# A two-MLP attention kernel: the second MLP takes its wide token groups first and its narrow one last

## The chip, the cores and the metric

The kernel runs on one core of one Trainium2 chip. The metric is the time of one execution on the device in microseconds (us); the median of several runs counts. A profiled execution gives the rows that are shown; its span, from the first to the last instruction, is a little shorter than its own time.

## The reference

Three stages follow each other; only the last one is touched by the change.

```python
def _moe2_ref(x, w1, w2, w3, w_out):
    h = np.maximum(np.maximum(x @ w1, x @ w2), x @ w3)
    return (h @ w_out).astype(np.float32)

def reference(...):
    attn_out = _attn_ref(q, k, v, g_norm)          # linear attention and a norm
    x = attn_out, as 4608 tokens of 512
    x = _moe_ref(x, ...)                           # 512 -> 2048 -> 512, relu squared
    return _moe2_ref(x, ...)                       # 512 -> 768 -> 512, maximum of three products
```

## The kernel before, in words

**Precision.** Every float32 operand of a large product is split into a high and a low part (hilo, line 90: a copy on ScalarE, a subtraction on VectorE), and each product is three matmuls: high by high, high by low, low by high.

**First MLP.** The 4608 tokens are nine tiles of 512 (numbers 0 to 8). A list of slots, one per tile and block of 128 hidden units, is walked in order (line 721). A slot runs u1 (line 337, 12 matmuls into a PSUM bank), u1_end (line 348, ScalarE and VectorE) and, two slots late, u2 (line 359, 12 matmuls into four PSUM banks). Attention for later tiles runs beside it and writes the token tiles xh and xl of pool xp, which has two buffers (x_tile, line 280). The last two tiles, 7 and 8, are walked in two halves of the hidden units: (7, first half), (8, first half), (7, second half), (8, second half). At the end of a half the four banks are added into four staging tiles of pool stp (line 373) and stored to DRAM (line 378, y_dr).

**Between the two.** From the slot where tile 8 begins, "more" (line 748) prepares the second MLP's weights: combine (line 406) makes nine weight tiles of 1792 KB in DRAM (wc_dr), and split_out (line 428) makes six tiles of w_out (wo_dr). They run one after the other through one set of buffers (pool cp), and their last part runs on beside the second MLP.

**Second MLP.** It works on five groups of tokens (SUPERS, line 385): before, the first group is tile 0 as two halves of 256 tokens (the narrow group), then come four groups of two tiles, two halves of 512 tokens each (the wide groups). Products of a pair of 2 by 2 blocks are formed with seven multiplications in place of eight (Winograd's form of Strassen's scheme). For each group there are
- token sums (tok_steps, line 446): 8 loads of y_dr, 14 splits and 8 subtractions, whose results T are read by all nine weight tiles of the group;
- nine steps v1 (line 496), one per weight tile wc: seven products of six matmuls, copies out of PSUM, additions and running maxima, and in every third step the splits of the hidden values hh, hl;
- v2 (line 563): one part per 128 tokens, each of 18 matmuls of width 512, then a copy and a store. The narrow group has four parts, a wide one eight. The first two parts are begun with four of the six hidden blocks, so that the last splits of v1 are covered.

pair_load (line 439) loads one weight tile; each v1 ends with the load for three steps later.

**What sets the order.** A scheduler fixes each engine's order of instructions when the kernel is built, by place in the program and by when it reckons an instruction to be ready. Each engine, and the queue of SP that issues nearly all DMAs, then keeps that order: an instruction whose wait is not over holds up all behind it. A tile that lands on bytes of a closed pool waits only for the users of the old tiles on its own bytes (reuse_waits="tile", line 49).

**Where the tiles lie before.** On the right side of SBUF, on the 64 KB of the first MLP's weights f < 8 (pool wpa, closed at line 752): two weight tiles wc (pool w2a), 14 token tiles (ta) and four load buffers (ya). So pair_load(0) and pair_load(1) are issued in the tail of the first MLP. The third weight tile (pool w2b) and the other token tiles (tb) lie on the left, on bytes that the first MLP holds to its end.

Of the kernel before, what the change touches and what calls it, by code (L numbers as in the profile page):

```python
# [8 lines left out]
F32 = mybir.dt.float32  # L9
F32R = mybir.dt.float32r  # L10
# [10 lines left out]
P = 128  # L21
# [3 lines left out]
def fused_kernel(ctx, tc, qt, kv, kvr, g_norm, w_in, w_out, s, b, w1, w2, w3, w_out2, out):  # L25
    nc = tc.nc
    B, NP, SM, _, _ = kv.shape
# [6 lines left out]
    KD = DM // P  # L34
    KF = DFF // P
    KM = DF2 // P
    TW = 512
    NTILE = NT // TW
# [9 lines left out]
    def pool(name, bufs, space=None, st=ctx, side="left"):  # L48
        kw = {"space": space} if space is not None else {"side": side, "reuse_waits": "tile"}
        return st.enter_context(tc.tile_pool(name=name, bufs=bufs, **kw))  # L50
# [10 lines left out]
    xp = pool("xp", 2, st=mlp1)  # L61
# [21 lines left out]
    HW = DM // 2  # L83
# [6 lines left out]
    def hilo(hi, lo, src):  # L90
        nc.scalar.activation(out=hi, in_=src, func=ACTF.Copy)  # L91
        nc.vector.tensor_tensor(out=lo, in0=src, in1=hi.bitcast(F32), op=ALU.subtract)  # L92


    def w_load(src):
        raw = rawp.tile([P, 2 * DM], U32, tag="raw", name="raw")
        dma(out=raw, in_=src)
        return raw
# [21 lines left out]
    class Weights:  # L120
# [6 lines left out]
        def load(self, cnt):  # L127
            while self.loaded < min(cnt, len(self.need)):
                self.raw[self.loaded] = w_load(self.need[self.loaded][0])
                self.loaded += 1  # L130
# [146 lines left out]
    x_t = {}  # L277
    held = []

    def x_tile(i):  # L280
        if i not in x_t:
            x_t[i] = (
                xp.tile([P, KD, TW], F32R, tag="xh", name="xh"),
                xp.tile([P, KD, TW], F32R, tag="xl", name="xl"),
            )
        return x_t[i]

    def put_x(p, g0, src, n):
        xh, xl = x_tile(g0 // TW)
        o = g0 % TW  # L290
        hilo(xh[:, p, o:o + n], xl[:, p, o:o + n], src)
# [31 lines left out]
    def flush_held():  # L323
        while held:
            p, g0, xo, n = held.pop(0)
            put_x(p, g0, xo[:, :n], n)
# [5 lines left out]
    def y_prev(t):  # L332
        for j in range(KD):
            prev[t, j] = stage()
            dma(out=prev[t, j], in_=y_dr[t][:, j, :])

    def u1(t, o, n, f):
        xh, xl = x_t[t]
        h = ps_h.tile([P, TW], F32, tag="h", name="h")
        w = wi[f].rearrange("p z (a c) -> p z a c", c=P)  # L340
        i = 0
        for kk in range(KD):
            for z, x in ((0, xh), (0, xl), (1, xh)):
                nc.tensor.matmul(h[:, :n], lhsT=w[:, z, kk, :], rhs=x[:, kk, o:o + n], start=(i == 0), stop=(i == 3 * KD - 1))  # L344
                i += 1
        return h
# [35 lines left out]

    A11, A12, A22, S1, S2, S3, S4 = range(7)
    POS = (2, 3, 1, 4, 5, 0, 6)
    SUPERS = [(0, TW // 2)] + [(t, TW) for t in range(1, NTILE, 2)]

    class Plain:

# [48 lines left out]
    wcs, w2p = {}, {}  # L437

    def pair_load(i):
        if i < len(SUPERS) * NQ:  # L440
            wcs[i] = w2p["b" if i % 3 == 2 else "a"].tile([P, 2, 7, HW], F32R, tag="wc", name="wc")
            dma(out=wcs[i].bitcast(F32), in_=wc_dr[i % NQ])

    tok = {}
# [1 line left out]
    def tok_steps(si):  # L446

        t, n = SUPERS[si]
        D2 = KD // 2
        where = ((y_dr[t], 0), (y_dr[t], n)) if n < TW else ((y_dr[t], 0), (y_dr[t + 1], 0))  # L450
        B, T = {}, {}
        tok[si] = T

        def load(nm, h, kk):
            y, o = where[h]
            k = kk + (D2 if nm[1] == "2" else 0)
            if n < TW and kk:
                B[nm, kk] = B[nm, "both"][:, n:2 * n]
            else:
                B[nm, "both"] = w2p["yb" if kk else "ya"].tile([P, TW], F32, tag="y", name="y2")  # L460
                B[nm, kk] = B[nm, "both"][:, :n]
            dma(out=B[nm, kk], in_=y[:, k, o:o + n])

        def split(nm, src, kk):
            if n < TW:
                p = w2p["ta"].tile([P, TW], F32R, tag="t", name=nm)
                hi, lo = p[:, :n], p[:, n:2 * n]
            else:
                home = w2p["tb" if len(T) < 7 else "ta"]
                hi = home.tile([P, TW], F32R, tag="t", name=nm + "h")  # L470
                lo = home.tile([P, TW], F32R, tag="t", name=nm + "l")
            hilo(hi, lo, B[src, kk])
            T[nm, kk] = (hi, lo)

        def sub(o, x, y, kk):
            nc.vector.tensor_tensor(out=B[o, kk], in0=B[x, kk], in1=B[y, kk], op=ALU.subtract)

        seq = []
        both = range(D2)
        for nm, h in (("b21", 0), ("b11", 0), ("b22", 1), ("b12", 1)):  # L480
            seq += [lambda kk=kk, nm=nm, h=h: load(nm, h, kk) for kk in both]
        for nm in ("b21", "b11", "b22"):
            seq += [lambda kk=kk, nm=nm: split(nm, nm, kk) for kk in both]
        for o, x, y in (("b11", "b12", "b11"), ("b12", "b22", "b12"), ("b22", "b22", "b11")):
            seq += [lambda kk=kk, o=o, x=x, y=y: sub(o, x, y, kk) for kk in both]
        for nm, src in (("t2", "b22"), ("t1", "b11")):
            seq += [lambda kk=kk, nm=nm, src=src: split(nm, src, kk) for kk in both]
        seq += [lambda kk=kk: sub("b21", "b21", "b22", kk) for kk in both]
        for nm, src in (("t4", "b21"), ("t3", "b12")):
            seq += [lambda kk=kk, nm=nm, src=src: split(nm, src, kk) for kk in both]  # L490
        return seq

    big = {}
    h2t = {}
# [1 line left out]
    def v1(si, q):  # L496

        n = SUPERS[si][1]
        w, T = wcs.pop(si * NQ + q), tok[si]
# [63 lines left out]
    def v2_steps(si):  # L563

        t, n = SUPERS[si]
        nb = 2 * n // P
# [154 lines left out]
    for i, sl in enumerate(slots):  # L721
        t, o, n, f, fa, fb = sl
        for gi, (b0, b1) in beside.items():
            if b0 == i:
                flush_held()
                todo = steps_of(*groups[gi])
                span, k_done, base = 2 * (b1 - b0), 0, 2 * i
        wa.to(max(sum(1 for d in due if d <= i + 1), wa.done + (1 if n == TW else 0)))
        if fa > 0 and f == fb - 1:
            y_prev(t)  # L730
        h = u1(t, o, n, f)
        for half in range(2):
            if half:
                if len(pend) == LAG:
                    u2(*pend.pop(0))
                pend.append((*sl, u1_end(h, n)))
            want = min(len(todo), -(-len(todo) * (2 * i + half + 1 - base) // span))
            while k_done < want:
                todo[k_done]()
                k_done += 1  # L740
        if early <= i < tail and (i - early) % 3 == 0:
            wq.step()
        if i == tail:
            while wq.done < len(wq.need):
                wq.step()
            attn.close()
            cp = pool("cp", 1, st=mlp1)
            more = [lambda q=q: combine(cp, q) for q in range(NQ)] + [lambda m=m: split_out(cp, m) for m in range(KM)]
        if i >= tail and (i - tail) % 3 < 2 and more:
            more.pop(0)()  # L750
        if i == tail + FA + LAG + 1:
            low.close()
            w2p["a"] = pool("w2a", 2, side="right")
            w2p["ta"] = pool("ta", 14, side="right")
            w2p["ya"] = pool("ya", 4, side="right")
            pair_load(0)
            pair_load(1)
            toks = tok_steps(0)
        if i > tail + FA + LAG + 5:
            for _ in range(3):  # L760
                if toks:
                    toks.pop(0)()
# [8 lines left out]
    w2p["x"] = pool("ps_x", 1, PSUM)  # L771
    w2p["s"] = pool("s2", 3)
    w2p["c"] = pool("c2", 8)
    w2p["b"] = pool("w2b", 1)
    w2p["yb"] = pool("yb", 4)
    w2p["tb"] = pool("tb", 14)
    w2p["h"] = pool("h2", 4 * KM)
    w2p["e"] = pool("e2", 2)
    wop = pool("wop", KM)
    pair_load(2)  # L780
    for m in range(KM):
        wob[m] = wop.tile([P, 2, DM], F32R, tag="wo", name="wo2")
        dma(out=wob[m].bitcast(F32), in_=wo_dr[m])
    toks = []
    for si in range(len(SUPERS)):
        for q in range(NQ):
            v1(si, q)
            if si == 0 and q >= 2:
                toks = toks or tok_steps(1)
                for fn in toks[3 * (q - 2):3 * (q - 1)]:  # L790
                    fn()
        seq = v2_steps(si)
        for fn in seq[:2]:
            fn()
        if si + 1 < len(SUPERS):
            for fn in (toks[21:] if si == 0 else tok_steps(si + 1)):
                fn()
        for fn in seq[2:]:
            fn()
# [57 lines left out]
```

## Time and profile before

| What | us |
|---|---|
| runs: median (lowest to highest of 3) | 1453.16 (1452.19 to 1454.43) |
| the profiled execution's own time | 1453.55 |
| its span | 1451.8 |
| TensorE (PE) busy | 1416.9 (98%) |
| VectorE (DVE) busy | 899.5 (62%) |
| ScalarE (ACT) busy | 617.1 (43%) |
| mean granted TensorE clock, as a share of 2.4 GHz | 0.995 |

How to read it: busy time is the union of an engine's instructions. Matmuls are pipelined, so PE counts as busy while one follows another; what a stage costs is read from the times at which its matmuls start. The second MLP runs from about 908 us to the end.

### The profile page before, as it was taken

To read this page: it belongs to the slowest core of one execution; us is meant where nothing else is said; L and a number is where in the kernel's file an instruction comes from. 1 tells how busy PE (TensorE), PEld (TensorE's weight loads), DVE (VectorE), ACT (ScalarE), POOL (GpSimd) and SP (SyncE) were. 2 spreads that over 40 slices of the span, in tenths; PEclk is the share of its full clock that TensorE was granted. 3 is DMA by queue.
4 is the path that set the end of the run, shared out by engine and by line. 5 is a ranking of instruction groups with operands and counts; after the bars stand their busy time and mean duration, and the time that the engine had idled before them with its cause. 6 is when DMAs were issued, how large, how long until landed. Compare 5 with 4: busy or idle time off the path is not lost.

```text
span 1451.8 us, 18930 instructions
## 1 busy us (share of the span) xinstructions
PE 1416.9 (98%) x7010; PEld 1172.8 (81%) x7010; DVE 899.5 (62%) x1722; ACT 617.1 (43%) x1255; POOL 12.1 (1%) x41
## 2 busy tenths in 40 slices
PE   6899989999999999999999999999999999999998
PEld 4678867888888888888888888988888888888887
DVE  6999998874455455454446556666564572673561
ACT  6664457454455455455544444332232241232221
POOL 1000000000000000000000000000000000000000
PEclk9999999999999999999999999999999999999999
DMA  6555565741111202111013788986553553552521
GB/s 213 176 182 194 169 203 183 244 131 37 44 47 46 73 14 74 45 47 44 15 48 123 240 311 304 367 339 234 189 197 138 187 209 126 188 196 82 185 96 58
DMA packets 67132, 217.77 MB, mean 150 GB/s; under 512 B 8032, under 2 KB 20320, under 8 KB 61280
## 3 DMA queue, kind: packets, MB, share of 16 engines
q1 hardware_dynamic: 66592, 216.56, 43.5%
q8 instruction: 55, 0.90, 0.2%
q14 instruction: 37, 0.30, 0.1%
q10 hardware_dynamic: 448, 0.00, 0.0%
HBM read 165.41 MB, written 51.12 MB: 149 GB/s over the span
## 4 chain that ended last, share of the span: by engine, by line
PE 83%; DVE 7%; DMA 6%; ACT 2%; issue 1%; SPq 0%; ACTq 0%; DVEq 0%
PE h L344 22%; PE y L367 22%; PE r L507 14%; PE x L507 11%; PE o L576 10%; DMA raw<-in_w_in 2%; DMA raw<-in_w 1%; PE ops L262 1%; PE kvps L225 1%; DMA F<-wf_dr 1%; DVE tb L109 1%; DVE w L92 1%; DMA wc<-wc_dr 1%; DVE r L354 1%; DMA raw<-in_w_out 1%
## 5 line engine op out<-in xcount | busy, mean ns | idle before, releaser
L344 PE MATMUL h<-xh,w 128*128 128x512 f32 (+1 forms) x1176 | 386.5, 389 | 3.3 <-ACT xh L91 2.1
L367 PE MATMUL y<-gh,w 128*128 128x512 f32 (+1 forms) x1176 | 384.8, 388 | 2.6 <-ACT gh L355 2.2
L344 PEld LDWEIGHTS h<-xh,w 128*128 128x128 f32 x1176 | 220.7, 189 | 50.1 <-ACT xh L91 4.1
L367 PEld LDWEIGHTS y<-gh,w 128*128 128x128 f32 x1176 | 221.5, 189 | 48.7 <-ACT gh L355 3.7
L344 PE MATMUL h<-xl,w 128*128 128x512 f32 (+1 forms) x588 | 228.4, 389 | 0.2 <-DVE xl L92 0.2
L367 PE MATMUL y<-gl,w 128*128 128x512 f32 (+1 forms) x588 | 228.6, 389 | 0.0
L356 DVE SCALAR_TENSOR_TENSOR gl<-r,cst,gh 128x512 fp32r<-128x512 f32 (+1 forms) x147 | 108.6, 739 | 122.1 <-ACT gh L355 121.2
L354 DVE SCALAR_TENSOR_TENSOR r<-r,cst 128x512 f32<-128x512 f32 (+1 forms) x147 | 108.6, 739 | 122.0 <-ACT r L353 121.5
L515 ACT ACTIVATE s<-x 128x512 f32<-128x512 f32 (+1 forms) x135 | 74.9, 555 | 237.7 <-PE x L507 236.4
L355 ACT ACTIVATE gh<-r,cst 128x512 fp32r<-128x512 f32 (+1 forms) x147 | 104.9, 713 | 149.7 <-PE y L367 138.9
L353 ACT ACTIVATE r<-h 128x512 f32<-128x512 f32 (+1 forms) x147 | 86.6, 589 | 164.4 <-PE h L344 142.5
L520 DVE TENSOR_TENSOR c<-r,s 128x512 f32<-128x512 f32 (+1 forms) x135 | 81.8, 634 | 82.4 <-ACT s L515 81.2
L576 PE MATMUL o<-wo,hh 128*128 128x512 f32 x432 | 132.6, 389 | 0.0
L367 PEld LDWEIGHTS y<-gl,w 128*128 128x128 f32 x588 | 111.5, 190 | 20.9 <-DVE gl L356 0.2
L344 PEld LDWEIGHTS h<-xl,w 128*128 128x128 f32 x588 | 110.9, 189 | 21.5 <-DVE xl L92 1.2
L576 PEld LDWEIGHTS o<-wo,hh 128*128 128x128 f32 x432 | 80.8, 188 | 16.7 <-ACT hh L91 0.2
L576 PE MATMUL o<-wo,hl 128*128 128x512 f32 x216 | 83.6, 389 | 0.0
L520 DVE TENSOR_TENSOR u<-r,s 128x512 f32<-128x512 f32 (+1 forms) x45 | 28.7, 637 | 65.8 <-PE r L507 65.7
L106 ACT ACTIVATE ta<-raw 128x512 f32<-128x512 f32 x56 | 37.6, 671 | 49.0 <-DMA raw<-in_w 17.4
L507 PE MATMUL r<-b21h,wc 128*128 128x512 f32 x144 | 50.4, 389 | 0.0
L507 PE MATMUL x<-t2h,wc 128*128 128x512 f32 x144 | 50.2, 389 | 0.0
L507 PE MATMUL r<-t1h,wc 128*128 128x512 f32 x144 | 50.2, 389 | 0.0
(140 smaller groups left out, 2050.0 us busy)
## 6 DMA issues: line engine op xcount, KB each, us to landing
wc<-wc_dr SPq DMA_DIRECT2D x45, 1792.0 KB, 7.4
kv<-in_kv SPq DMA_DIRECT2D x32, 512.0 KB, 5.3
y_dr<-st SPq DMA_DIRECT2D x56, 256.0 KB, 3.4
raw<-in_w_out SPq DMA_DIRECT2D x22, 512.0 KB, 3.6
raw<-in_w SPq DMA_DIRECT2D x18, 512.0 KB, 3.9
out<-e SPq DMA_DIRECT2D x36, 256.0 KB, 2.0
raw<-in_w_in SPq DMA_DIRECT2D x16, 512.0 KB, 4.1
y<-y_dr SPq DMA_DIRECT2D x32, 256.0 KB, 4.9
```

What stands on the lines that cost most here:

```text
L92: nc.vector.tensor_tensor(out=lo, in0=src, in1=hi.bitcast(F32), op=ALU.subtract)
L106: nc.scalar.activation(out=af, in_=high.bitcast(F32), func=ACTF.Abs)
L344: nc.tensor.matmul(h[:, :n], lhsT=w[:, z, kk, :], rhs=x[:, kk, o:o + n], start=(i == 0), stop=(i == 3 * KD - 1))
L353: nc.scalar.activation(out=rn, in_=h[:, :n], func=ACTF.Relu)
L354: nc.vector.scalar_tensor_tensor(out=rn, in0=rn, scalar=sb_sb[:, 0:1], in1=rn, op0=ALU.mult, op1=ALU.mult)
L355: nc.scalar.activation(out=gh[:, :n], in_=rn, func=ACTF.Identity, bias=sb_sb[:, 1:2])
L356: nc.vector.scalar_tensor_tensor(out=gl[:, :n], in0=rn, scalar=sb_sb[:, 1:2], in1=gh[:, :n].bitcast(F32), op0=ALU.add, op1=ALU.subtract)
L367: nc.tensor.matmul(yt[t, o][j][:, :n], lhsT=w[:, z, c], rhs=r[:, :n], start=(f == fa and i == 0), stop=(f == fb - 1 and i == 2))
L507: nc.tensor.matmul(ps, lhsT=w[:, z, POS[c], kk * P:(kk + 1) * P], rhs=x, start=(first and i == 0), stop=(i == 3 * KD // 2 - 1), skip_group ...
L515: nc.scalar.activation(out=t, in_=ps, func=ACTF.Copy)
L520: nc.vector.tensor_tensor(out=o, in0=ps, in1=t, op=ALU.add)
L576: nc.tensor.matmul(acc[b], lhsT=l[:, o:o + P], rhs=wob[m][:, z, :], start=(m == 0 and i == 0), stop=(m == KM - 1 and i == 2))
```

## The change

1. The first MLP's two token tiles xh and xl become one tile x of two parts, in the same pool with two buffers.
2. SUPERS lists the four wide groups first and the narrow group (tile 8) last.
3. All three weight tiles wc lie in one pool w2 on the left side, opened when the first MLP's pools close; the early pair_load(0) and pair_load(1) in the first MLP's tail go, and all three loads stand behind line 768. The pool e2 moves ahead of w2.
4. The right side's 64 KB now hold both sets of token tiles (ta and tb, 14 each) and the four load buffers ya. The first group's token sums run through ya in two halves (kk = 0 in full, then kk = 1), so the second half's loads wait for the first half's buffers. For later groups the steps alternate between kk = 0 and 1 as before.
5. The special handling that ran the second group's token sums inside the narrow group's v1 steps goes: each group's token sums now run between the first parts of v2 of the group before.

```diff
     def x_tile(i):
         if i not in x_t:
-            x_t[i] = (
-                xp.tile([P, KD, TW], F32R, tag="xh", name="xh"),
-                xp.tile([P, KD, TW], F32R, tag="xl", name="xl"),
-            )
+            t = xp.tile([P, 2, KD, TW], F32R, tag="x", name="x")
+            x_t[i] = (t[:, 0], t[:, 1])
         return x_t[i]
...
-    SUPERS = [(0, TW // 2)] + [(t, TW) for t in range(1, NTILE, 2)]
+    SUPERS = [(t, TW) for t in range(0, NTILE - 1, 2)] + [(NTILE - 1, TW // 2)]
...
-            wcs[i] = w2p["b" if i % 3 == 2 else "a"].tile([P, 2, 7, HW], F32R, tag="wc", name="wc")
+            wcs[i] = w2p["w"].tile([P, 2, 7, HW], F32R, tag="wc", name="wc")
...
-                B[nm, "both"] = w2p["yb" if kk else "ya"].tile([P, TW], F32, tag="y", name="y2")
+                B[nm, "both"] = w2p["yb" if kk and si else "ya"].tile([P, TW], F32, tag="y", name="y2")
...
+        every = [list(of(kk)) for kk in range(D2)]
+        return sum(every, []) if si == 0 else [fn for fns in zip(*every) for fn in fns]
...
             low.close()
-            w2p["a"] = pool("w2a", 2, side="right")
             w2p["ta"] = pool("ta", 14, side="right")
+            w2p["tb"] = pool("tb", 14, side="right")
             w2p["ya"] = pool("ya", 4, side="right")
-            pair_load(0)
-            pair_load(1)
             toks = tok_steps(0)
...
     w2p["c"] = pool("c2", 8)
-    w2p["b"] = pool("w2b", 1)
     w2p["yb"] = pool("yb", 4)
-    w2p["tb"] = pool("tb", 14)
+    w2p["e"] = pool("e2", 2)
+    w2p["w"] = pool("w2", 3)
     w2p["h"] = pool("h2", 4 * KM)
-    w2p["e"] = pool("e2", 2)
     wop = pool("wop", KM)
-    pair_load(2)
+    for i in range(3):
+        pair_load(i)
...
-    toks = []
     for si in range(len(SUPERS)):
         for q in range(NQ):
             v1(si, q)
-            if si == 0 and q >= 2:
-                toks = toks or tok_steps(1)
-                for fn in toks[3 * (q - 2):3 * (q - 1)]:
-                    fn()
         seq = v2_steps(si)
         for fn in seq[:2]:
             fn()
         if si + 1 < len(SUPERS):
-            for fn in (toks[21:] if si == 0 else tok_steps(si + 1)):
+            for fn in tok_steps(si + 1):
                 fn()
```

## Rows read from the trace of the kernel before

**Rows 1.** The page, part 1, TensorE and the other engines over the span.
```profile
PE 1416.9 (98%) x7010; PEld 1172.8 (81%) x7010; DVE 899.5 (62%) x1722; ACT 617.1 (43%) x1255; POOL 12.1 (1%) x41
```

**Rows 2.** TensorE's timeline: start us, us, line, operation; first matmuls of groups.
```profile
908.11 0.88 PE L507 MATMUL r<-b,wc 128*128 128x256 f32 x6
...
1060.22 0.62 PE L576 MATMUL o<-wo,hh 128*128 128x512 f32 x2
...
1092.89 0.39 PE L507 MATMUL r<-b21h,wc 128*128 128x512 f32 x1
...
1211.23 0.39 PE L507 MATMUL r<-b21h,wc 128*128 128x512 f32 x1
```

**Rows 3.** TensorE's timeline, narrow group: first product of seven of its v1 steps.
```profile
913.14 0.88 PE L507 MATMUL r<-b,wc 128*128 128x256 f32 x6
...
918.98 0.98 PE L507 MATMUL r<-b,wc 128*128 128x256 f32 x6 [0.61 <-DVE u L553]
...
924.12 0.88 PE L507 MATMUL r<-b,wc 128*128 128x256 f32 x6
...
929.65 0.97 PE L507 MATMUL r<-b,wc 128*128 128x256 f32 x6
...
936.04 0.95 PE L507 MATMUL r<-b,wc 128*128 128x256 f32 x6 [1.10 <-DMA wc<-wc_dr]
...
957.41 0.98 PE L507 MATMUL r<-b,wc 128*128 128x256 f32 x6
...
963.71 0.98 PE L507 MATMUL r<-b,wc 128*128 128x256 f32 x6 [0.42 <-DVE u L553]
```

**Rows 4.** VectorE's timeline, narrow group: wide token work and the additions behind it.
```profile
917.91 0.68 DVE L92 TENSOR_TENSOR b21l<-y,b21h 128x512 fp32r<-128x512 f32 x1
918.51 0.42 DVE L553 TENSOR_TENSOR u<-r,u 128x256 f32<-128x256 f32 x1
...
961.45 1.41 DVE L476 TENSOR_TENSOR y<-y,y 128x512 f32<-128x512 f32 x2
...
963.23 0.42 DVE L553 TENSOR_TENSOR u<-r,u 128x256 f32<-128x256 f32 x1
```

**Rows 5.** TensorE's timeline: the last matmul that reads the tokens of tile 8.
```profile
899.72 0.39 PE L344 MATMUL h<-xh,w 128*128 128x512 f32 x1
```

**Rows 6.** SP's timeline: DMA issues around the end of the first MLP.
```profile
886.87 3.98 SPq L462 DMA_DIRECT2D y<-y_dr  x4
...
900.47 0.40 SPq L442 DMA_DIRECT2D wc<-wc_dr  x1
...
906.98 1.68 SPq L378 DMA_DIRECT2D y_dr<-st  x3
910.92 0.32 SPq L434 DMA_DIRECT2D wo_dr<-ohi  x1
...
912.51 0.44 SPq L378 DMA_DIRECT2D y_dr<-st  x1
...
927.35 5.19 SPq L783 DMA_DIRECT2D wo<-wo_dr  x6
```

**Rows 7.** Line 378, the last four stores: issue to landing, first three, then the fourth.
```profile
DMA to landing us min/median/max: 4.0/4.1/4.2
DMA to landing us min/median/max: 4.4/4.4/4.4
```

**Rows 8.** Line 442, weight loads of 1100 to 1400 us: issue to landing.
```profile
DMA to landing us min/median/max: 7.0/7.3/8.2
```

**Rows 9.** Stretches: length, PE, PEld, DVE, ACT, POOL busy (instructions), PEclk, DMA share, GB/s.
```profile
890.00:908.00 18.00, 18.00 (x81) 14.92 (x80) 8.00 (x12) 5.08 (x8) 0.00 (x0) 1.00 0.82 279
936.00:941.00 5.00, 4.96 (x41) 4.99 (x42) 3.08 (x9) 1.07 (x3) 0.00 (x0) 1.00 1.03 419
200.00:205.00 5.00, 4.27 (x12) 3.00 (x10) 4.01 (x11) 2.45 (x7) 0.15 (x1) 0.66 0.87 249
```

**Rows 10.** TensorE's timeline ahead of 200 us: the longest wait there.
```profile
198.92 0.80 PE L225 MATMUL kvps<-kv 128*64 128x64 f32 x20 [2.77 <-ACT og L272]
```

More of the change, by code (lines that the diff above doesn't have):

```diff
@@ L476, in sub, with of @@
             nc.vector.tensor_tensor(out=B[o, kk], in0=B[x, kk], in1=B[y, kk], op=ALU.subtract)
[L478 to L491, printed above, removed]
+        def of(kk):
+            for nm, h in (("b21", 0), ("b11", 0), ("b22", 1), ("b12", 1)):
+                yield lambda nm=nm, h=h: load(nm, h, kk)
+            for nm in ("b21", "b11", "b22"):
+                yield lambda nm=nm: split(nm, nm, kk)
+            for o, x, y in (("b11", "b12", "b11"), ("b12", "b22", "b12"), ("b22", "b22", "b11")):
+                yield lambda o=o, x=x, y=y: sub(o, x, y, kk)
+            for nm, src in (("t2", "b22"), ("t1", "b11")):
+                yield lambda nm=nm, src=src: split(nm, src, kk)
+            yield lambda: sub("b21", "b21", "b22", kk)
+            for nm, src in (("t4", "b21"), ("t3", "b12")):
+                yield lambda nm=nm, src=src: split(nm, src, kk)
+        every = [list(of(kk)) for kk in range(D2)]
+        return sum(every, []) if si == 0 else [fn for fns in zip(*every) for fn in fns]
     big = {}
```

## The prediction, made before the changed kernel ran

> **What bounds the kernel now.** I read the page's busy table first: TensorE is busy 98% of the span [rows 1], so only time in which it waits, or works for nothing, can be won. Then its timeline at the group borders, to price the second MLP. A wide group takes 1211.23 − 1092.89 = 118.34 us. Its v2 takes 1092.89 − 1060.22 = 32.67 us for 8 × 18 = 144 matmuls, 0.227 us each, and its nine v1 steps the other 85.67, 9.52 us each [rows 2]. The narrow group and the first wide one together take 1092.89 − 908.11 = 184.78 us, which leaves 66.44 for the narrow one. An undisturbed narrow step takes 913.14 − 908.11 = 5.03 us [rows 2, 3]; nine steps and half of a wide group's v2 are 45.27 + 16.33 = 61.6 us. **So 4.8 us are lost in the narrow group**, and that is all the change can win in that place: 0.33% of the time. About 0.2%, 2.9 us, is what a measurement of this kernel can tell from no change.
>
> Where they are lost: TensorE waits 1.10 us for a weight tile at 936.04, while the DMA engines move 419 GB/s [rows 3, 9], and it waits for VectorE, 0.61 us at 918.98 and 0.42 at 963.71 [rows 3]. VectorE is late there because wide token work of the next group stands ahead of the addition that frees the PSUM bank: a split of 0.68 us at 917.91, two subtractions of 1.41 at 961.45 [rows 4]. The step from 957.41 to 963.71 takes 6.30 us instead of 5.03 [rows 3].
>
> **Narrow group last (gain).** The wide token work and the loads of w_out (927.35, [rows 6]) then fall into wide stages, and no next group's tokens stand beside the narrow steps. What stays is the narrow steps' own friction. The three steps from 918.98 on (to 924.12, to 929.65, and to 936.04 less its wait of 1.10) have no wide token work beside them and take 5.14, 5.53 and at most 5.29: 0.11, 0.50 and up to 0.26 over 5.03 [rows 3]. The 0.50 comes after a step with splits, which happens twice in nine. I estimate 2 × 0.5 + 5 × 0.12 = 1.6 us left (bounds: 0.5, if VectorE alone was late, and 4.8, if all of it is the group's own). **Gain 4.8 − 1.6 = 3.2 us.** Weights keep up: each load has two narrow steps, 10.06 us, from the release of its buffer to its use, and takes 7.0 to 8.2 us when little else moves [rows 8]; 1792 KB per step (1.835 MB) at 419 GB/s are 4.4 us, under 5.03. At the very end the first two parts of v2 (24 matmuls, 5.4 us) cover the last splits as for the wide group before; the last copy and store are the same. Nothing there.
>
> **Weights on the left (loss).** Counting bytes of the pools in order of opening, the first weight tile lies 34 to 48 KB behind the constants, inside the second buffer of x. With x as one tile that buffer holds tile 7 alone. Its last reader stands eight slots ahead of tile 8's, which is at 899.72 [rows 5]; at 24 matmuls of 0.227 us a slot that is about 856, and even if the load goes only when tile 8 is done, as the third weight tile's does now (issued 900.47, [rows 6]), it lands 7.3 to 8.2 us later, at the start of the second MLP. No loss. The merge itself adds no instruction.
>
> The second weight tile covers 48 to 62 KB: the buffers of gh and gl, read until 908.11, and three of the four staging buffers of y. Its load must wait for three stores to land. They issue from 906.98, the third by about 908.3, and take 4.0 to 4.2 us [rows 6, 7]: 912.4. SP's queue at that time stands behind a split of w_out until 910.92 and passes on at 912.5 [rows 6]. So the load goes at 912.5 to 913 and lands 7.3 to 8.2 us later [rows 8], about 920.4. TensorE wants it after one wide step, at 908.11 + 9.52 = 917.63. **Stall 2.8 us** (bounds: 1.0, if SP is free at once and the load takes 7.0; 7.1, if it must wait for the fourth store, issued 912.51 and landing 4.4 later, at 916.9 [rows 6, 7], then some 7.8, between 7.3 and 8.2 [rows 8]). The third tile needs the fourth staging buffer and first-MLP weights, so it goes near 917 and lands by 926 even behind the second; it is wanted at 920.4 + 9.5 = 930. Covered. Behind these waits on SP's queue stand the last w_out pieces and the loads of w_out, wanted only when v2 begins, near 996, against 927.35 now: 60 us of cover. The removed early loads free the DMA engines in the first MLP's tail, where TensorE loses nothing (18.00 of 18.00 us busy, [rows 9]).
>
> **A stall and the clock.** Ahead of 200 us TensorE waited 2.77 us at 198.92 [rows 10], and from 200 to 205 its granted clock was 0.66 [rows 9]: 0.34 × 5 / 0.5 = 3.4 us at 1.2 instead of 2.4 GHz, so 1.7 us of work lost. After the wait of 1.10 us at 936.04 [rows 3] it stayed at 1.00 [rows 9]. The stall forecast lies at the upper of the two, but single and between dense matmuls, where the 198.92 wait had thin attention work around it; so I take no drop, and keep 1.7 us as a rival. The Trainium skill (TensorE: Matmul & The Clock Gate, section HAM oscillation — how this bites in real kernels) says that a matrix engine left idle by a DMA wait may be set back to its low clock and begin the next work cold. By that rule the sum below would be 1.7 us higher.
>
> **Wide tokens in the first MLP's tail.** The first group's token sums are now wide: 14 splits of 0.68 and 8 subtractions of 0.70 us on VectorE [rows 4], 15.1 us. The second half, 7.6 us, must wait for the first half's load buffers, which come free about when they do now, near 887, where four loads go [rows 6]. VectorE is busy 8.00 of 18.00 us from 890 to 908 [rows 9], so 10 us are free; and the second half is wanted product by product over 8 us behind 908. Nothing lost, if the loads go by about 893; if they come 5 us later, up to 4 us (bounds 0 and 4). Later groups' sums run in the 32.67 us of v2 [rows 2] as for three groups now. The crosswise use of ta and tb delays the first of them by some products, within that cover.
>
> **Sum.** Against the profiled execution's 1453.55: −4.8 + 1.6 + 2.8 = −0.4, so 1453.15. The median of the runs, 1453.16, stands 0.39 below that execution; against it **1452.8 us**.
>
> **The rivals.**
> 1. Faster: the second weight tile is (nearly) in time, because its bytes don't meet the last staging buffers or the stores land sooner, so that stall and friction together stay under 1.9 us. For it: one wide step is 9.52 us long, more than a load takes [rows 2, 8]. Against: the staging buffers lie behind x in the same stack. 1453.2 − 4.8 + 1.2 = 1449.6. Chance 0.14.
> 2. Slower: that load stands behind the fourth store, which SP itself holds back until 912.51 [rows 6]. Stall 7.1, with the clock's drop 8.8: 1453.2 − 3.2 + 7.1 = 1457.1, or 1458.8. It decides once the stall passes 3.2 + 2.9 = 6.1 us, that is, if the load goes later than about 916. For it: SP keeps its order. Against: the buffers go round in fours, so the fourth store's buffer is the third tile's. Chance 0.13.
> 3. The forecast's stall, and the clock falls: 1452.8 + 1.7 = 1454.5, no change. Chance 0.12.
> 4. The narrow group keeps its waits wherever it stands, so the change doesn't win what it reorders for: 1453.2 + 2.8 = 1456.0, at the edge of no change. Chance 0.06.
> 5. The second half of the first group's tokens comes late: 1452.8 + 4 = 1456.8. Chance 0.05.
>
> **How the numbers follow.** The forecast keeps 0.50; its own range, with friction 0.5 to 2.5 and a stall of 1.5 to 4.5 us, is 1450.3 to 1455.4. Faster by over 0.2% (under 1450.3): rival 1, 0.14. Slower (over 1456.1): rival 2, rival 5 and a third of rival 4, 0.20. The rest, 0.66, is no change. The range reaches to rivals 1 and 2: 1449.5 to 1457.3.
>
> **What would show it.** In the changed profile: TensorE waiting some 2.8 us once, for wc, near 917.6, and nowhere else for weights; the second weight load issued near 913 behind the stores of line 378; narrow steps at 5.03 to 5.5 us and the narrow group near 63 us, ending the kernel; wide groups at 118.3; a granted clock of 1.00 behind the stall. Wrong would be no wait at the second step (rival 1), one over 6 us (rival 2), a first product waiting for a token split, or a DMA wait in the narrow steps.

## The result and the profile after

The changed kernel takes **1468.61 us** (median of four runs, 1466.22 to 1472.76), the kernel before 1453.06 beside it. The ratio is 1.0101, with a 95% interval of 1.0083 to 1.0119: some 15 us slower where 1452.8 was forecast and 1457.3 was the upper end of the range. The profiled execution is the one of 1466.22 us, with a span of 1464.4 us. Line numbers of the changed kernel are one or two lower than before: the weight loads stand in line 440, the products of the second MLP in line 506, the stores of y in 376.

Three lines of the page and of its list of waits show nearly all of it: TensorE's busy time, the group of first products of the second MLP with its idle time and the releaser, and the wait for weights (total, times, longest).

```profile
PE 1416.0 (97%) x7010; PEld 1173.0 (80%) x7010; DVE 899.6 (61%) x1722; ACT 616.9 (42%) x1255; POOL 11.9 (1%) x41
...
L506 PE MATMUL r<-b21h,wc 128*128 128x512 f32 x144 | 51.2, 397 | 16.0 <-DMA wc<-wc_dr 16.0
...
PE r L506 <- DMA wc<-wc_dr: 16.0, 1, 16.0
```

TensorE is as busy as before [rows 1] and waits 16.0 us, once. TensorE's timeline places it (start, length, operation, and in brackets the idle time ahead with its releaser): the last product of the first MLP, the first of the second, the first of the second step, and the group borders.

```profile
906.51 0.39 PE L365 MATMUL y<-gh,w 128*128 128x512 f32 x1
922.90 0.77 PE L506 MATMUL r<-b21h,wc 128*128 128x512 f32 x1 [16.01 <-DMA wc<-wc_dr]
...
934.15 0.39 PE L506 MATMUL r<-b21h,wc 128*128 128x512 f32 x1
...
1043.00 0.39 PE L506 MATMUL r<-b21h,wc 128*128 128x512 f32 x1
...
1161.34 0.39 PE L506 MATMUL r<-b21h,wc 128*128 128x512 f32 x1
...
1397.98 0.88 PE L506 MATMUL r<-b,wc 128*128 128x256 f32 x6
...
1403.02 0.88 PE L506 MATMUL r<-b,wc 128*128 128x256 f32 x6
...
1460.37 0.39 PE L575 MATMUL o<-wo,hl 128*128 128x512 f32 x1
```

So the wait stands at the **first** weight tile, not at the second, where 2.8 us had been forecast. The first step then takes 934.15 − 922.90 = 11.25 us instead of 9.52 [rows 2]; the second and all later wide steps take 9.52. A wide group takes 1161.34 − 1043.00 = 118.34 us, as before [rows 2]. The narrow group, now last, takes from 1397.98 to 1460.60 (its last matmul, 0.23 us after it begins): 62.62 us, where it took 66.44. With the first MLP ending at 906.74 instead of 908.11, the spans balance: +16.0 + 1.8 (first wide group, 120.10 us) − 3.8 − 1.4 = +12.6, and 1464.4 − 1451.8 = 12.6.

SP's timeline shows why the tile is late: `y_dr<-st` are the last stores of the first MLP, `wo_dr<-ohi` and `olo` a piece of w_out split by ScalarE and VectorE, `wc<-wc_dr` the weight loads. The last line is of the list of DMA issues (tile, queue, operation, count, KB each, median us to landing), for the two loads issued first.

```profile
906.45 1.79 SPq L376 DMA_DIRECT2D y_dr<-st  x3
911.27 0.32 SPq L432 DMA_DIRECT2D wo_dr<-ohi  x1
912.00 0.32 SPq L433 DMA_DIRECT2D wo_dr<-olo  x1
912.37 0.43 SPq L376 DMA_DIRECT2D y_dr<-st  x1
912.85 0.44 SPq L460 DMA_DIRECT2D y<-y_dr  x1
913.39 0.40 SPq L780 DMA_DIRECT2D wo<-wo_dr  x1
913.83 2.44 SPq L440 DMA_DIRECT2D wc<-wc_dr  x3
916.37 2.60 SPq L780 DMA_DIRECT2D wo<-wo_dr  x5
...
wc<-wc_dr SPq DMA_DIRECT2D x2, 1792.0 KB, 10.8
```

All three weight loads go together, at 913.83 and after, behind the fourth store. The forecast had the first by 900.5. SP's list of waits from 908 to 917 us (who waited for what: total, times, longest) tells what held them:

```profile
SPq L432 <- ACT ohi L91: 3.0, 1, 3.0
SPq L440 <- DMA y_dr<-st: 1.1, 1, 1.1
```

SP stood 3.0 us for ScalarE's split of w_out, with the fourth store and the three loads behind it. Of the loads only the third, at 915.96, then waited for a store. The first went 1.46 us after the fourth store was issued, and that store took 3.5 us to land: it waited for none, and was late by its place in SP's order alone. Of TensorE's 16.0 us, 913.83 − 906.74 = 7.1 lie ahead of the issue; the other 8.9 are the load itself. The windows of that stretch (length, busy time of PE, PEld, DVE, ACT and POOL with their instructions, granted clock, DMA share, GB/s) show the clock:

```profile
910.00:915.00 5.00, 0.00 (x0) 0.00 (x0) 0.69 (x1) 0.63 (x1) 0.00 (x0) 0.50 0.77 268
...
920.00:925.00 5.00, 2.10 (x5) 1.76 (x6) 0.00 (x0) 0.00 (x0) 0.00 (x0) 0.50 1.00 430
925.00:930.00 5.00, 5.00 (x20) 4.05 (x20) 0.69 (x1) 0.60 (x1) 0.00 (x0) 0.87 1.02 439
930.00:935.00 5.00, 5.00 (x24) 4.14 (x23) 1.40 (x3) 1.20 (x2) 0.00 (x0) 1.00 0.99 399
```

It is at 0.50 (1.2 GHz) while TensorE waits and for the first products after: 11.25 − 9.52 = 1.7 us of work lost.

### The profile page after: what moved, and what is told of

It reads as the page before. It is cut to its first block, busy times and chain, and to the rows that moved or that the text cites. A ratio compares the mean times of both kernels' runs of the same rounds, so it can differ in the third digit from the quotient of the medians.

```text
span 1464.4 us, 18934 instructions
## 1 busy us (share of the span) xinstructions
PE 1416.0 (97%) x7010; PEld 1173.0 (80%) x7010; DVE 899.6 (61%) x1722; ACT 616.9 (42%) x1255; POOL 11.9 (1%) x41
## 4 chain that ended last, share of the span: by engine, by line
PE 80%; DMA 8%; DVE 7%; ACT 2%; issue 1%; SPq 0%; ACTq 0%; DVEq 0%
PE h L342 20%; PE y L365 20%; PE r L506 15%; PE x L506 11%; PE o L575 10%; DMA F<-wf_dr 2%; DMA raw<-in_w 2%; DMA raw<-in_w_in 2%; PE ops L262 1%; PE kvps L225 1%; DMA raw<-in_w_out 1%; DVE tb L109 1%; DVE r L352 1%; DVE w L92 1%; DMA wc<-wc_dr 1%
## 5 line engine op out<-in xcount | busy, mean ns | idle before, releaser
L342 PE MATMUL h<-x,w 128*128 128x512 f32 (+1 forms) x1764 | 423.8, 388 | 4.1 <-ACT x L91 2.7
L342 PEld LDWEIGHTS h<-x,w 128*128 128x128 f32 x1764 | 323.3, 188 | 71.5 <-ACT x L91 4.3
L506 PE MATMUL x<-b11h,wc 128*128 128x512 f32 x144 | 50.4, 391 | 0.0
L506 PE MATMUL r<-b22h,wc 128*128 128x512 f32 x144 | 50.2, 389 | 0.0
```

Source lines behind the costliest of these rows:

```text
L506: nc.tensor.matmul(ps, lhsT=w[:, z, POS[c], kk * P:(kk + 1) * P], rhs=x, start=(first and i == 0), stop=(i == 3 * KD // 2 - 1), skip_group ...
```

## Experiments

Open after this: are the bytes of the first tile really in use until 913, as a rival to my count would have it, or are they free and the load merely stands late in SP's order? My theory of the second kind: buffers of one pool come free together, so the first tile's load stands behind the users of what its pool's other tiles overlap. The next three kernels split pools, one more each time; four others move or undo parts.

What such a split keeps can be read from the addresses in the built kernels. The first weight tile has the same bytes in the changed kernel and in all three. The second and the third trade places: in the changed kernel the second lies on the last of the three places (62 to 76 KB by the prediction's count) and the third on the middle one (48 to 62 KB), in the three others it is the other way round. So the three kernels compare the first load on unchanged bytes, but not the second.

**Three pools for the weights**

```
+ wcs[i] = w2p["w", i % 3].tile(...)
...
- w2p["w"] = pool("w2", 3)
+ for i in range(3):
+     w2p["w", i] = pool(f"w2{i}", 1)
```

> The changed kernel with one edit: the three weight tiles stand in three pools of one buffer each, opened one behind the other, so every tile keeps its bytes. Theory A (the loads were late because the buffers of one pool of three come free together, when the last old user of any byte of the pool is done, and the first load therefore stands behind the last stores and two loads of w_out in SP's queue; the first tile's own bytes were free long before): the first load goes at about 902 us beside the last loads of y tokens, and lands 8 to 9 us later; TensorE's first wait on wc falls from 16.0 to 3 us or so, the second load goes near 914 and costs another 2 to 3 us at the second step; the clock's 1.7 us are mostly gone. Time 1468.6 - 17.7 + 5.5 = 1456.4 us, between 1454 and 1460. Theory B (the bytes of the first tile are in use until about 913 us, as laid out): same bytes, same wait of 16 us, 1468.6 us, within 2. Theory C (the load can go early, but the DMA engines are too busy in the first MLP's tail to bring it): first load issued near 902, landed not before 918, time over 1464.

Measured: 1461.53 us (1459.07 to 1462.55), 1.0050 of the kernel before (1.0036 to 1.0064). SP's timeline, the landing of the fourth store (issued 915.44), then TensorE's two waits:

```profile
902.87 0.41 SPq L440 DMA_DIRECT2D wc<-wc_dr  x1
...
915.44 0.45 SPq L376 DMA_DIRECT2D y_dr<-st  x1
...
918.51 0.80 SPq L440 DMA_DIRECT2D wc<-wc_dr  x2
...
DMA to landing us min/median/max: 2.9/2.9/2.9
...
911.49 0.47 PE L506 MATMUL r<-b21h,wc 128*128 128x512 f32 x1 [3.72 <-DMA wc<-wc_dr]
...
927.87 0.77 PE L506 MATMUL r<-b21h,wc 128*128 128x512 f32 x1 [4.96 <-DMA wc<-wc_dr]
```

On the same bytes the first load goes 11 us sooner, at the place theory A named, and its wait falls from 16.0 to 3.7 us. Theories B and C fall. The time is 1.5 us over A's range: the second load goes at 918.51, not at 914, and costs 4.96 us. That one is held by its own bytes: on the middle place lies the buffer of the fourth store, and the load goes when that store has landed, 2.9 us after 915.44. And one thing was still odd: the first tile lies on the buffer of x's tile 7, done near 856, yet its load went at 902.87, behind the last read of tile 8.

**x in two pools as well**

```
- xp = pool("xp", 2, st=mlp1)
+ xps = [pool(f"xp{i}", 1, st=mlp1) for i in range(2)]
...
+ t = xps[i % 2].tile(...)
```

> The kernel with three weight pools of one buffer, with one more edit: the two buffers of x stand in two pools of one buffer each, on the same bytes. Theory A, made sharper by the runs so far (a new buffer is given out when every buffer of each old pool that it touches has been left): the first weight tile lies on tile 7's buffer alone, and in the kernel with three pools it still went at 902.87 us, just behind the last read of tile 8; now it goes when tile 7 is done, near 856 us, and TensorE doesn't wait at the start of the second MLP. The second load stays behind the fourth store of y and the last split of w_out, near 918, lands some 9 us later and is wanted at 917 to 918.5: a lone wait of 8 to 10.5 us, and some 2 us of low clock behind it: 1449.0 + 9.5 + 2 = 1460.5 us, 1458 to 1463. Theory B (only each byte's own last reader counts, and the 902 of the kernel before came from SP being busy): the first load stays near 902 and its wait at 3.7 us, 1461.5 us; the two differ in the trace, not in the time.

Measured: 1459.69 us (1456.75 to 1461.67), 1.0039 (1.0025 to 1.0052). Again SP's timeline, and TensorE's only wait for weights:

```profile
861.39 0.38 SPq L440 DMA_DIRECT2D wc<-wc_dr  x1
...
913.81 0.45 SPq L376 DMA_DIRECT2D y_dr<-st  x1
917.27 0.32 SPq L432 DMA_DIRECT2D wo_dr<-ohi  x1
917.77 0.32 SPq L440 DMA_DIRECT2D wc<-wc_dr  x1
...
925.79 0.76 PE L506 MATMUL r<-b21h,wc 128*128 128x512 f32 x1 [7.34 <-DMA wc<-wc_dr]
```

The first load moves from 902.87 to 861.39 and TensorE's wait for it is gone: the rule holds for the old pool too. All buffers of an old pool that the new pool touches count, not just those under the tile. They count in the order that is set when the kernel is built, not as a wait on the chip: the built kernels give this load the same wait with and without this edit, for the last matmul that reads tile 7 (near 855.7 us in both). At 902.87 it had been free to go for 47 us. Theory B falls. The lone wait is 7.34 us, a little under the range of 8 to 10.5, since the first step itself took longer (next kernel).

**The staging buffers in four pools: the state that the prediction assumed**

```
- stp = pool("stp", 4, st=mlp1)
+ stps = [pool(f"stp{i}", 1, st=mlp1) for i in range(4)]
...
+ staged.append(0)
+ return stps[(len(staged) - 1) % 4].tile(...)
```

The edit does a second thing: the staging buffers now go round strictly in turn, which moves the fourth store's buffer from the middle place (the second tile's here) to the last one (the third's). Only with that is the state the one that the prediction took for granted.

> As the kernel with x in two pools, and y's four staging buffers also in four pools of one buffer each, on the same bytes. This is the state of things that the prediction took for granted: the first weight tile follows tile 7, the second follows three stores of y and not four. Theory A: the second load goes near 913 to 914 us, lands 8 to 9 us later, near 922, and is wanted at 917 to 918.5: one lone wait of 3.5 to 5 us. If such a wait lowers the clock as the waits of 3.7 and 5.0 us did: 1449.0 + 4.3 + 2 = 1455.3 us, 1453 to 1457.5; if it doesn't, as the prediction had it, 1453.3, and 1452 with its wait of 2.8. Rival (the four stores were not what held the second load): it stays near 918, and the time near 1460.

Measured: 1456.35 us (1453.65 to 1458.67), 1.0018 (1.0006 to 1.0029). SP's timeline, the landing of the second load, TensorE's two waits in the first step and behind it, and the windows (columns as above; line numbers are two higher here):

```profile
912.35 0.44 SPq L378 DMA_DIRECT2D y_dr<-st  x1
912.96 0.32 SPq L442 DMA_DIRECT2D wc<-wc_dr  x1
...
917.27 0.32 SPq L442 DMA_DIRECT2D wc<-wc_dr  x1
917.63 7.65 SPq L783 DMA_DIRECT2D wo<-wo_dr  x3
...
wc<-wc_dr SPq DMA_DIRECT2D x1, 1792.0 KB, 10.2
...
911.27 0.50 PE L508 MATMUL x<-t2h,wc 128*128 128x512 f32 x1 [0.88 <-ACT s L516]
...
923.31 0.77 PE L508 MATMUL r<-b21h,wc 128*128 128x512 f32 x1 [6.29 <-DMA wc<-wc_dr]
...
920.00:925.00 5.00, 1.69 (x4) 1.44 (x5) 0.18 (x1) 0.00 (x0) 0.00 (x0) 0.58 1.00 412
925.00:930.00 5.00, 5.00 (x18) 3.96 (x18) 0.69 (x1) 0.60 (x1) 0.00 (x0) 0.74 0.99 404
```

Here the second load goes at 912.96: "at 912.5 to 913", as the forecast put it, once its three stores are all that lies under it. Whether the split of the pool of four had a part in that, beside the moved buffer, this kernel can't tell. What was wrong in that step is the load's length: 10.2 us to landing, not 7.8, so the wait is 6.29 and not 2.8 (nor the 3.5 to 5 that I expected now). The third weight load (917.27) and w_out (917.63) are moved beside it, at 412 GB/s; [rows 8] are from a quiet stretch. That these two stretch it is argued from the rows, not tried alone. The clock falls (0.58, 0.74), and the next step takes 934.96 − 923.31 = 11.65 us, 2.1 too long. The 0.88 us at 911.27 is ScalarE, a split of w_out ahead of the copy that TensorE needs.

**The weight tiles opened first**

```
  w2p["x"] = pool("ps_x", 1, PSUM)
+ w2p["w", 0] = pool("w20", 1)
+ w2p["w", 1] = pool("w21", 1)
  w2p["s"] = pool("s2", 3)
  w2p["c"] = pool("c2", 8)
+ w2p["w", 2] = pool("w22", 1)
...
- w2p["w"] = pool("w2", 3)
```

> The changed kernel with the three weight tiles in pools of their own, two of them opened ahead of every other pool of the second MLP and the third behind c2, so that they lie on bytes that the attention's and the first MLP's last buffers leave early. Theory A: the first load goes over 100 us ahead, the second by 901, the third by 913, all ahead of the loads of w_out; TensorE doesn't wait for wc at all. What is left of the change is the narrow group's gain of 3.2 to 3.5 us and a border some 1.4 us shorter: 1468.6 - 16.0 - 1.7 = 1450.9 by the medians, 1448.5 by the profiled executions; between 1447.5 and 1452. Theory B (the weights on the left cost what they cost because of the transfers around them, not because of where and when they are issued): a wait of several us stays at the start of the second MLP, 1455 or more.

Measured: **1449.03 us** (1448.31 to 1452.17, seven runs), 0.9975 of the kernel before (0.9964 to 0.9986). It beats both kernels. SP's timeline, and TensorE's only wait of over 0.5 us at the start of the second MLP:

```profile
788.82 0.41 SPq L440 DMA_DIRECT2D wc<-wc_dr  x1
...
901.83 0.40 SPq L440 DMA_DIRECT2D wc<-wc_dr  x1
...
918.60 0.69 SPq L440 DMA_DIRECT2D wc<-wc_dr  x1
...
919.53 0.50 PE L506 MATMUL r<-b21h,wc 128*128 128x512 f32 x1 [0.57 <-DVE u L552]
```

The third load goes later than expected (918.60, not 913), and is still in time for a step that begins near 929. So the weights on the left cost nothing where their loads stand early enough in the queue, and theory B falls.

**One pool of three, opened first**

```
  w2p["x"] = pool("ps_x", 1, PSUM)
+ w2p["w"] = pool("w2", 3)
  w2p["s"] = pool("s2", 3)
...
- w2p["w"] = pool("w2", 3)
```

> The changed kernel with its one pool of three weight tiles, but opened as the first pool of the second MLP, on bytes that are all left earlier than those it has in the changed kernel. Theory A (the three buffers come free together, with the last old user of any byte of the pool): the first load goes with the last old user of those bytes, at about 902 us, not earlier, though part of the bytes is free 100 us before; it lands at about 910, TensorE waits some 3 us and perhaps 2 to 3 us more at the second step: 1454 to 1458 us. Theory B (each buffer by its own bytes): the first load goes near 780, the second and the third as in the kernel with pools of their own; no wait, 1448 to 1452 us.

Measured: 1456.62 us (1454.12 to 1461.60), 1.0021 (1.0009 to 1.0033). SP's timeline, TensorE's waits and the windows:

```profile
905.46 0.44 SPq L440 DMA_DIRECT2D wc<-wc_dr  x1
...
913.86 0.47 PE L506 MATMUL r<-b21h,wc 128*128 128x512 f32 x1 [3.58 <-DMA wc<-wc_dr]
...
926.61 0.76 PE L506 MATMUL r<-b21h,wc 128*128 128x512 f32 x1 [2.95 <-DMA wc<-wc_dr]
...
910.00:915.00 5.00, 1.42 (x7) 1.00 (x6) 1.68 (x3) 0.00 (x0) 0.00 (x0) 1.00 0.94 340
915.00:920.00 5.00, 5.00 (x24) 4.12 (x23) 1.39 (x2) 1.62 (x3) 0.00 (x0) 1.00 1.03 345
...
925.00:930.00 5.00, 3.39 (x8) 2.74 (x9) 1.81 (x4) 0.00 (x0) 0.00 (x0) 0.59 0.99 421
```

The first load goes at 905.46 and not at 788.82, though the first tile lies on the very same bytes as in the kernel just before: theory A again, within its range. (The rows are those of the profiled execution, which took 1461.60 us, 5 more than the median.)

**The narrow group first, on that memory**

```
- SUPERS = [(t, TW) for t in range(0, NTILE - 1, 2)] + [(NTILE - 1, TW // 2)]
+ SUPERS = [(0, TW // 2)] + [(t, TW) for t in range(1, NTILE, 2)]
```

and the narrow group's token work spread over its steps as in the kernel before.

> The memory of the kernel with the weight tiles opened first, but with the group of 512 tokens first and its token work spread as in the kernel before. This isolates what the order of the groups is worth where weights don't hold it. Theory A (the order gains what was forecast, 3.2 us, or the 3.5 that the trace of the changed kernel shows): slower than the kernel with the weight tiles first by 3 to 4 us, near 1453. Rival (the order gains nothing by itself, what the traces show is the weights' doing): the same time as that kernel within 1 us. A narrow step needs its weights after 5 us instead of 9.5, so a wait for the second or third tile can add 1 to 5 us: those are read off the trace and taken out.

Measured: 1453.74 us (1452.59 to 1456.96), 1.0006 (0.9997 to 1.0015) of the kernel before, and 4.7 us over the kernel with the weight tiles first. TensorE's waits for weights, and one window:

```profile
919.10 1.07 PE L506 MATMUL r<-b,wc 128*128 128x256 f32 x6 [1.89 <-DMA wc<-wc_dr]
...
937.82 0.95 PE L506 MATMUL r<-b,wc 128*128 128x256 f32 x6 [0.36 <-DMA wc<-wc_dr]
...
920.00:925.00 5.00, 5.00 (x32) 5.00 (x32) 1.73 (x5) 1.18 (x3) 0.00 (x0) 0.68 0.98 408
```

Undoing the order gives the gain back, so the order is worth it. But the expectation asked to take weight waits out, and here they are most of it: 1.89 + 0.36, and 0.32 × 5 = 1.6 us of work lost at the low clock, make 3.9. The narrow group takes 67.8 us here (906.95 to 974.77) and 62.9 in the kernel with the weight tiles first. (The groups are compared, since the two profiled executions, 1453.67 and 1452.17, differ at the end of the first MLP as well.) Without those 3.9 us they would be 1 us apart. On this memory, then, narrow-last wins mostly because steps of 5 us no longer ask for weights while the border's transfers run, and only partly because VectorE has no wide tokens beside them. That is read from the rows, not tried.

**The merge of x's halves alone**, in the kernel before (`x_tile` as in the change, nothing else).

> The kernel before with one part of the change: x's two halves as one tile. No instruction is added. As forecast: no change, within 0.2% of the kernel before. Rival: one tile makes the first MLP's products wait for the second half's last write, or gives its buffer back later, at each of nine tiles: 1 to 5 us slower, with waits at line 342's or 344's matmuls in the trace.

Measured: 1453.87 us (1452.44 to 1455.75), 0.9999 (0.9989 to 1.0009). No change; the merge costs nothing, and the rival falls.

## Why the prediction was wrong

- **The step that failed** is "Weights on the left", the first weight tile: "even if the load goes only when tile 8 is done ... No loss." The bytes were counted rightly: the tile lies on tile 7's buffer. But I priced it by the last reader of its bytes alone, as if it would go when nothing held it. Its place in SP's order was later. The three tiles are one pool, and in that order its loads stood behind the last users of all old pools under any of the three: behind a split of w_out (911.27) and the fourth store (912.37). The first was issued at 913.83, with nothing left to wait for, 13 us behind the 900.47 taken for the worst case, and took 8.9 us instead of up to 8.2. Splitting pools moved this load, on unchanged bytes, to 902.87 and then to 861.39: that is the proof that the grouping decides. How the scheduler comes to its order is read off from these moves only. The range missed because this step had one value and no upper bound.
- **The second tile's stall** of 2.8 us didn't show, because the first tile came later still. Its bytes were counted wrongly too: the second tile got the last place and the third the middle one, where the buffer of the fourth store lay. In the state assumed, the issue time was right (912.96) and the load mis-sized: 10.2 us, and a wait of 6.3.
- **"I take no drop" of the clock** was wrong: 1.7 us were lost after the wait of 16.0 us. That rival 3 had the same 1.7 is in part luck, since it came from a much shorter wait (2.77 us, [rows 10]) and the runs here lost from 1.6 to 3.0 after most of their waits. The Trainium skill (TensorE: Matmul & The Clock Gate, section HAM oscillation — how this bites in real kernels) says that an engine left idle by a DMA wait may begin its next work at the low clock; the 0.50 in the windows above agrees.
- **Rival 2** had the right mechanism, a load behind the fourth store in an SP queue that keeps its order, but at the second tile, where a wide step covers most of it. At the first nothing does, and 7.1 became 16.0. What was held against it, that the fourth store's buffer is the third tile's, doesn't hold for the place it was said of: on the middle place (three pools) the second load did wait for that store.
- **The narrow group** was right: 62.6 us for a forecast of 63.2, so 1.0 us of friction where 1.6 was taken, and a first step of 1403.02 − 1397.98 = 5.04 us where 5.03 is the undisturbed one. How it was explained is only in part borne out. In the kernel before, the narrow steps waited 1.10 us for a weight and 1.03 for VectorE [rows 3]; in the changed kernel they wait for neither. On the other memory, with the narrow group first, weight waits and the clock weighed more than VectorE's wide work.
- **Right as well**: wide groups at 118.34 us; no wait for a token split, so rival 5 fell; no loss from the merge. The forecast's gain was there all along: without the weights' lateness the changed kernel is 0.25% faster than the one before.

## What to carry to other kernels

A load need not go when the last user of its bytes is done: that is only what it waits for on the chip. Price it as well by its place in the queue that issues it, which here followed the last user of everything that its pool, and the pools under it, share; the later of the two counts. Don't count on a pool handing out its buffers in the order of their addresses: read the addresses of the built kernel. Tiles that are wanted at different times belong in pools of their own, the one wanted first on the bytes that are left first. Give a load that "can't be late" an upper bound like any other term, taken from the queue it stands in.

## What was not expected of the hardware

The cost of the low clock didn't grow with the wait ahead of it: 1.7 us after 16.0 us, 1.9 after 7.34, 2.1 after 6.29, 2.7 after 4.96, 1.9 after 3.72, 1.6 after 1.89, but 3.0 after 2.95 (the step from 926.61 to 939.10 took 12.49 us), which came one step behind another wait of 3.58. That one, alone of those over 1.5 us, cost hardly anything: the clock read 1.00 in the window around 913.86 and in the next. What decides it is not settled here.

The end of the first MLP also moved between profiles, from 906.16 to 910.11 us, in kernels that are the same up to there or nearly so; times here are compared by medians, and stages from that end on.
